# Moving four precomputed weight sums between VectorE and GpSimd, and undoing a split product, in an attention + GEGLU kernel

## The chip, the cores and the metric

The kernel runs on one core of one Trainium2 chip. A core has TensorE (PE, matrix products into PSUM), VectorE (DVE), ScalarE (ACT), GpSimd (POOL), and SyncE (SP), which issues most of the transfers. The engines run side by side, each through its own list of instructions in a fixed order, and wait for each other by semaphores. The metric is the device time of one execution in microseconds. Beside it there is one profiled execution, from which all durations here are taken; its positions are microseconds from the start of its span.

## The reference

Eight batches of attention whose softmax stands on q (over the head's 64 columns) and on k (over the sequence), so that no sequence x sequence matrix arises, and then a gated feed-forward block on the result:

```
q_s = softmax(q, axis=-1);  k_s = softmax(k, axis=2)     # (8, 8, 576, 64)
kv  = einsum('bhsd,bhse->bhde', k_s, v)
x   = einsum('bhsd,bhde->bhse', q_s, kv)                  # -> (4608, 512)
out = (gelu(x @ w_gate) * (x @ w_val)) @ w_out            # 512 -> 1536 -> 512
```

Inputs and output are float32; the kernel multiplies in float16 and adds up in float32.

## The kernel before

**Tiling.** The work goes in nine blocks of 512 rows of x: blocks 0 to 7 are the first 512 of the 576 rows of each batch, and a block 8 (called B) gathers the remaining 64 rows of every batch. The order is 0 to 6, then 8, then 7. x is kept transposed, as `xt` (4 groups of 128 columns by 512 rows). The 1536 hidden columns are 12 groups of 128 (`fi`), and the gated result is `ht`.

**Products.** Blocks 0 and 1 compute gate and value plainly (`ffn_fi`): four matmuls of 512 columns into `psg`, four into `psv`, then GELU on ScalarE (line 471) and the gating on VectorE (line 472), which writes `ht`. From block 2 on, the hidden groups 0 to 5 use Strassen's scheme in Winograd's form (`product_gv`, line 605: seven products instead of eight), and the others stay plain. The output product is plain in block 0 (`mm_out`), and in Winograd's form from block 1 on (`out_strassen` with `product`, line 712).

**Sums for Winograd's form.** They need sums of quarters of each factor, all in float16 in SBUF:

- `sum_w(i)`, line 556: four sums of quarters of w_out into `tw1` to `tw4`, each 128 x 1536 elements, made once. `tw2` reads `tw1`, `tw4` reads `tw2`; `tw3` reads w_out alone. Product 5 reads `tw1`, product 6 `tw2`, product 7 `tw3`, product 4 `tw4`.
- `sum_wgv(nm, i)`, line 586: the same for w_gate and w_val, 128 x 768 elements each. Sums 1, 2 and 4 go to `ws`; sum 3 is written in place into the weights (`wg_sb`, `wv_sb`), which is allowed only once the plain products of block 1 have read these columns for the last time; block 2's seventh product reads them.
- `sum_h`, line 575: the sums of `ht` in each block (`sh`, `s4`, and one in place in `ht`).

**The output stage of block 1.** `out_strassen` runs products 1, 2, 5, 6, 3, 7 and 4 of 12 matmuls with 256 columns each, in three PSUM tiles `psa`, `psb`, `psc`. Between them VectorE scales `psa` or `psc` into SBUF (`snap`, line 744) and adds them into the output tile `yo` (`add`, line 750). Product 4 is added into `psa` after the last add has read it. At fixed places the stage takes in work for other blocks: at place (1, NS, 2), between products 6 and 3, the `kv` products of block 2 (`pskv`, line 342; normalised on VectorE, lines 346 and 348) and the casts of v of batch 3 on GpSimd (line 188); at place (1, NS, 4), in front of product 4, x of block 2 (`unit_x4`, lines 429 and 439), evacuated by ScalarE and VectorE (lines 190 and 192) into `xt` and `xtr`. The first gate product of block 2 reads `xt` right after product 4.

**What sets the order.** Nothing is planned by a scheduler: each engine's order is the order of the calls. A table `plan`, filled by `at(block, kind, index, ...)`, names the places. `ride` calls what stands at a place: FI is a step of the hidden groups of blocks 0 and 1, NS a step of the output stage, PR a step of the later blocks. At NS 17 of block 0, in its last output rows, stand `sum_w(1)` and `sum_w(3)` on GpSimd; at FI 4 of block 1 `sum_w(2)` and `sum_w(4)` on VectorE; at FI 11 of block 1 both in-place sums on GpSimd. The local value `cut` in `out_strassen` splits product 3: in blocks 1 to 5 its last group of `ht` (two matmuls) comes after product 7.

Of the kernel before, what the change touches and what calls it, by code (L numbers as in the profile page):

```python
# [18 lines left out]
def kernel(  # L19
# [10 lines left out]
    nc = tc.nc  # L30

    B, H, S, D = q.shape
# [4 lines left out]
    NFI = F // P  # L37
# [11 lines left out]
    NO = NFI // 2  # L49
# [30 lines left out]
    def big(shape, dt, name, hold=False, seed=False):  # L80
        tag = ring.pop(next(i for i, x in enumerate(ring) if x in full) if seed else 0)
        t = ps_big.tile(shape, dt, name=name, tag=tag)
        words = 1
        for n in shape[1:]:
            words *= n
        (full.add if words == 512 and shape[0] == 128 and dt == f32 else full.discard)(tag)
        if hold:
            held[id(t)] = (t, tag)
        else:
            ring.append(tag)  # L90
        return t

    def let_go(t):
        ring.append(held.pop(id(t))[1])
# [26 lines left out]
    for i, nm in enumerate("gv"):  # L121
        n = 3 * NO * P
# [442 lines left out]
    def sum_h(j0, j1, which, eng="dve"):  # L565
        step = 1 if j1 - j0 == 2 else NO // 2
        js, ks = slice(j0, j1, step), slice(NO + j0, NO + j1, step)
        a11, a21 = ht[:, js, 0:256], ht[:, js, 256:512]
        a12, a22 = ht[:, ks, 0:256], ht[:, ks, 256:512]
        s1, s2 = sh[1][:, js], sh[2][:, js]  # L570
        for i in which:
            o, a, b, op = {1: (s1, a21, a22, ALU.add), 2: (s2, s1, a11, ALU.subtract),
                           3: (a21, a11, a21, ALU.subtract),
                           4: (s4[:, js], a12, s2, ALU.subtract)}[i]
            (nc.gpsimd if eng == "pool" else nc.vector).tensor_tensor(out=o, in0=a, in1=b, op=op)  # L575

    def sum_wgv(nm, i, k=0, n=NO // 2, eng="dve"):
        w = wg_sb if nm == "g" else wv_sb  # L580
        lo, hi = slice(k * P, (k + n) * P), slice((k + NO // 2) * P, (k + NO // 2 + n) * P)
        a11, a21, a12, a22 = w[:, 0:2, lo], w[:, 0:2, hi], w[:, 2:4, lo], w[:, 2:4, hi]
        t = [ws[(nm, k // NO)][:, j, :, k % NO * P:(k % NO + n) * P] for j in range(3)]
        o, a, b, op = {1: (t[0], a21, a22, ALU.add), 2: (t[1], t[0], a11, ALU.subtract),
                       3: (a21, a11, a21, ALU.subtract), 4: (t[2], a12, t[1], ALU.subtract)}[i]
        (nc.gpsimd if eng == "pool" else nc.vector).tensor_tensor(out=o, in0=a, in1=b, op=op)

    def sum_x(xt, xs=xs):
        b11, b12, b21, b22 = (xt[:, c:c + 2, r:r + 256] for c in (0, 2) for r in (0, 256))
# [112 lines left out]
    def product(i, ps, first, ts=(0, 1), js=range(NO)):  # L702
        for j in js:
            for t in ts:
                c0, c1 = slice(t * P, (t + 1) * P), slice(256 + t * P, 256 + (t + 1) * P)
                a = {1: ht[:, j, c0], 2: ht[:, NO + j, c0], 3: s4[:, j, c0], 4: ht[:, NO + j, c1],
                     5: sh[1][:, j, c0], 6: sh[2][:, j, c0], 7: ht[:, j, c1]}[i]
                w = {1: wo_sb[:, j, 0:256], 2: wo_sb[:, NO + j, 0:256],
                     3: wo_sb[:, NO + j, 256:512]}.get(i)
                if w is None:  # L710
                    w = tw[{4: 4, 5: 1, 6: 2, 7: 3}[i]][:, j]
                nc.tensor.matmul(ps[t], a, w, start=(first and j == js[0] and (  # L712
                    t == ts[0] or ps[t].tensor is not ps[ts[0]].tensor)),
                                 stop=(j == js[-1]), skip_group_check=True)

    def get_x(b):
        return get_xt(b) if b < B else xtr

    def last_js(b):
        return (NO - 2 if b < 2 else NO // 2 - 1, NO)  # L720

    def out_strassen(b, last):
        yo = [yop.tile([P, 2, C], f32, name="yo", tag="yo") for _ in range(2)]
        c = (slice(0, 256), slice(256, 512))
        ps, tiles_ = {}, {}

        def get(nm):
            if last:
                tiles_[nm] = [big([P, 256], f32, "ps" + nm, True) for _ in range(2)]
                ps[nm] = [x for x in tiles_[nm]]  # L730
            else:
                tiles_[nm] = [big([P, 2, 256], f32, "ps" + nm, True)]
                ps[nm] = [tiles_[nm][0][:, t] for t in range(2)]

        def parts(nm):
            return [(0, ps[nm][0]), (1, ps[nm][1])] if last else [(slice(0, 2), tiles_[nm][0])]

        def snap(nm):
            sn = ffn.tile([P, 2, 256], f32, name="sn", tag="gl")
            for n, (t, src) in enumerate(parts(nm)):  # L740
                if n:
                    nc.scalar.activation(out=sn[:, t], in_=src, func=ACTF.Copy, scale=1.0 / _H_SCALE)
                else:
                    nc.vector.tensor_scalar(out=sn[:, t], in0=src, scalar1=1.0 / _H_SCALE,
                                            scalar2=None, op0=ALU.mult)
            return sn

        def add(nm, sn, half, col):
            for t, src in parts(nm):
                nc.vector.scalar_tensor_tensor(  # L750
                    out=yo[half][:, t, c[col]], in0=src, scalar=1.0 / _H_SCALE,
                    in1=sn[:, t], op0=ALU.mult, op1=ALU.add)

        js = (0, 1, 2, 3, 4, 5) if b < 2 else (0, 3, 1, 4, 2, 5)
        get("a")
        product(1, ps["a"], True, js=js[:4])
        ride(b, NS, 0)
        if b >= B - 1:
            pair_step(b, get_x(b), NFI - NO // 2 - 1, 4)
        ride(b, PR, "e")  # L760
        get("b")
        product(1, ps["a"], False, js=js[4:])
        sum_h(*last_js(b), (1, 2))
        s1 = snap("a")
        product(2, ps["b"], True, js=js)
        add("b", s1, 0, 0)
        for x in tiles_["b"]:
            let_go(x)
        sum_h(*last_js(b), (4,), "pool" if b > 1 else "dve")
        get("c")  # L770
        product(5, ps["c"], True, js=js)
        sum_h(*last_js(b), (3,), "pool" if b > 1 else "dve")
        s5 = snap("c")
        ride(b, NS, 1)
        product(6, ps["a"], False, js=js)
        s2 = snap("a")
        ride(b, NS, 2)
        cut = NO - 1 if b < B - 2 else NO
        product(3, ps["c"], False, js=js[:cut])
        if cut < NO:  # L780
            product(7, ps["a"], False, js=js)
            add("a", s5, 1, 1)
            product(3, ps["c"], False, js=js[cut:])
        add("c", s2, 0, 1)
        for x in tiles_["c"]:
            let_go(x)
        store_rows(b, 0, yo[0])
        if last:
            finish_last(b, ps["a"], yo[1], s5)
            return  # L790
        if cut == NO:
            product(7, ps["a"], False, js=js)
            add("a", s5, 1, 1)
        ride(b, NS, 4)
        if b == B:
            go_on(B - 1, get_x(B - 1), 1)
        product(4, ps["a"], False, js=js)
        nc.scalar.activation(out=yo[1][:, :, c[0]], in_=tiles_["a"][0], func=ACTF.Copy,
                             scale=1.0 / _H_SCALE)
        let_go(tiles_["a"][0])  # L800
        store_rows(b, 1, yo[1])
# [97 lines left out]
    FI, NS, PR = range(3)  # L899
    plan = {}  # L900

    def at(b, kind, i, *fns):
        plan.setdefault((b, kind, i), []).extend(fns)

    L = lambda f, *a: (lambda: f(*a))

    def load_2nd():
# [6 lines left out]
    at(0, NS, 5, L(unit_t, 1, 0))  # L914
    at(0, NS, 16, L(unit_kv, 1, 0), L(cast_v, 1, 4, 8), L(load_batch, 2, ((v, "v"),)),
       L(norm, 1, 3))
    at(0, NS, 17, L(unit_x, 1, 0, "act", True), L(unit_x, 1, 1, "act", True), L(sum_w, 1, "pool"),
       L(sum_w, 3, "pool"))
    at(0, NS, 7, L(exp, "q", 2))
    first1 = [[L(unit_t, 1, 1), L(unit_kv, 1, 1)],  # L920
              [L(unit_x, 1, 2, "dve"), L(preload, ACTF.Gelu)],
# [8 lines left out]

    at(1, FI, 2, L(unit_trem, 1))
    at(1, FI, 3, L(norm, 2, 2, "pool"), L(load_batch, 3, ((q, "q"), (k, "k"))))
    at(1, FI, 4, L(exp, "k", 2, 0, 4), L(norm, 2, 3, "pool"), L(sum_w, 2), L(sum_w, 4), make_s)
    at(1, FI, 5, L(cast_v, 2, 0, H))
    at(1, FI, 8, L(unit_td, 2))
    at(1, FI, 11, L(exp, "k", 2, 4, 8), L(exp, "q", 3))
# [3 lines left out]
    load_2 = lambda n: load_batch(n, ((v, "v"), (q, "q"), (k, "k")))  # L940
    for i, x in enumerate(("g1", "v1", "g2", "v2", "g4", "v4")):
        at(0, FI, 5 + i, L(sum_wgv, x[0], int(x[1])))
    at(1, FI, NFI - 1, L(sum_wgv, "g", 3, 0, NO // 2, "pool"), L(sum_wgv, "v", 3, 0, NO // 2, "pool"))
    for b in range(2, B):
        n = b + 1
        if n < B:
# [10 lines left out]
    for b in range(2, B - 1):  # L957
        n = b + 1
# [16 lines left out]
    def ride(b, kind, i):  # L975
        for fn in plan.get((b, kind, i), []):
            fn()

    for b in order:
# [16 lines left out]
        if b == 0:  # L996
# [5 lines left out]
            for ns in range(4):  # L1002
                cut = 9 if ns == 2 else 7 if ns == 3 else NFI
# [37 lines left out]
```

The softmax here doesn't subtract the row's maximum and nothing guards it: scores larger than these inputs give would overflow.

## Time and profile before

| | us |
|---|---|
| median of 4 runs (297.27 to 297.55) | 297.37 |
| the profiled execution | 297.45 |
| its span, first to last instruction | 295.5 |
| TensorE busy / VectorE / GpSimd / ScalarE | 286.0 / 220.9 / 200.4 / 181.9 |
| TensorE, VectorE busy from 60 to 71 us (block 1's hidden groups) | 11.00, 10.82 |
| TensorE, VectorE, GpSimd busy from 71 to 76 us (block 1's output) | 4.75, 4.81, 0.00 |
| TensorE, VectorE, GpSimd busy from 76 to 84 us (to block 2's start) | 7.78, 6.26, 4.50 |

The granted clock of TensorE is 1.00 in all these stretches. A line of the timeline reads: start, duration, engine, line of the kernel, operation, output<-inputs by name, shapes, count of merged instructions, and in brackets the idle time of the engine in front of it with what ended it. Successive instructions of one engine overlap a little in the records[...]. A matmul's record includes its drain: in a row of matmuls the distance from start to start is the pace.

### The profile page before, as it was taken

What the parts mean: (1) busy time and instruction counts of PE and PEld (TensorE: products, weight loads), DVE (VectorE), ACT (ScalarE), POOL (GpSimd) and SP (SyncE); (2) the same over time, 40 slices, a digit from 0 to 9 for tenths busy, and PEclk for the clock granted to TensorE, in tenths of its full rate; (3) what the DMA queues carried; (4) which work ended last, traced back from release to release, by engine and by line L of the source; (5) the groups of instructions that cost most, each with busy time, mean ns of one, the idle gap of its engine ahead of it and who ended that gap; (6) DMA issues with size and microseconds to landing.
All of it is one profiled execution on the core that took longest, in us unless ns stands there. A gap on an engine that the chain in (4) does not pass through costs nothing. (4 is left out here: it accounts for less than half of the span.)

```text
span 295.5 us, 6184 instructions
## 1 busy us (share of the span) xinstructions
PE 286.0 (97%) x2401; PEld 198.5 (67%) x2401; DVE 220.9 (75%) x409; ACT 181.9 (62%) x295; POOL 200.4 (68%) x181
## 2 busy tenths in 40 slices
PE   3999999999999999999999999999999999999994
PEld 1544445445866686668666866687667888888884
DVE  2955779999778677867777676777677788958892
ACT  3763367776676668667756966695662477327640
POOL 1557747894386877687768776967886366673770
PEclk9999999999999999999999999999999999999999
DMA  6999999998069504980399029901140110033003
GB/s 220 373 382 389 400 391 392 329 325 231 3 211 389 113 3 156 364 192 3 137 347 246 2 97 342 274 2 73 71 89 12 71 74 2 1 73 71 2 0 144
DMA packets 54621, 51.72 MB, mean 175 GB/s; under 512 B 18496, under 2 KB 50496, under 8 KB 54592
## 3 DMA queue, kind: packets, MB, share of 16 engines
q1 hardware_dynamic: 52864, 49.49, 52.8%
q10 hardware_dynamic: 1728, 1.84, 1.9%
q8 instruction: 19, 0.31, 0.4%
q14 instruction: 10, 0.08, 0.1%
HBM read 37.75 MB, written 9.44 MB: 160 GB/s over the span
## 5 line engine op out<-in xcount | busy, mean ns | idle before, releaser
L466 PE MATMUL psg<-xt,wg_sb 128*128 128x512 f16 x216 | 57.8, 379 | 0.2 <-DVE xt L192 0.2
L466 PE MATMUL psv<-xt,wv_sb 128*128 128x512 f16 x216 | 57.4, 379 | 0.0
L249 POOL TENSOR_TENSOR eq<-eq,rrq 128x640 f16<-128x640 f16 (+1 forms) x27 | 34.7, 1304 | 19.7 <-DVE rrq L242 16.1
L712 PEld LDWEIGHTS <-ht 128*128 128x128 f16 x384 | 36.5, 98 | 8.8 <-issue 2.5
L466 PEld LDWEIGHTS <-wv_sb 128*128 128x128 f16 x216 | 21.0, 98 | 20.5 <-issue 1.2
L466 PEld LDWEIGHTS <-wg_sb 128*128 128x128 f16 x216 | 21.1, 98 | 18.6 <-issue 0.2
L575 POOL TENSOR_TENSOR s<-ht,sh 128x512 f16<-128x512 f16 x21 | 25.3, 1206 | 9.5 <-DVE sh L575 9.5
L575 POOL TENSOR_TENSOR ht<-ht 128x512 f16<-128x512 f16 x21 | 25.2, 1199 | 5.5 <-DVE sh L575 5.5
L605 PEld LDWEIGHTS <-wv_sb 128*128 128x128 f16 x216 | 20.9, 98 | 11.2 <-issue 1.8
L188 POOL CAST v<-vt 128x640 f16<-128x640 f32 x26 | 20.7, 839 | 8.7 <-PE pskv L342 7.1
L650 POOL TENSOR_TENSOR ht<-eq 128x512 f16<-128x512 f32 x12 | 15.4, 1283 | 16.0 <-ACT eq L648 15.8
L471 ACT ACTIVATE gl<-psg 128x512 f32<-128x512 f32 x24 | 13.8, 597 | 16.6 <-PE psg L466 14.2
L630 ACT ACTIVATE glq<-pgb 128x256 f32<-128x256 f32 x27 | 10.2, 379 | 21.9 <-PE pgb L605 14.0
L712 PE MATMUL psa<-tw,ht 128*128 128x256 f16 x192 | 23.4, 272 | 0.0
L212 ACT ACTIVATE ek<-kt 128x1280 f16<-128x1280 f32 (+1 forms) x11 | 19.1, 1748 | 6.1 <-DMA kt<-in_k_dram 4.1
L605 PEld LDWEIGHTS <-wg_sb 128*128 128x128 f16 x216 | 21.1, 98 | 2.5
L660 ACT COPY pgb<-pga 128x512 f32<-128x512 f32 x27 | 15.8, 584 | 9.8 <-PE pga L605 9.5
L472 DVE SCALAR_TENSOR_TENSOR ht<-psv,gl 128x512 f16<-128x512 f32 x24 | 16.0, 683 | 7.2 <-PE psv L466 7.2
L622 ACT ACTIVATE gl<-psg 128x512 f32<-128x512 f32 x30 | 17.7, 589 | 5.7 <-PE psg L466 5.7
L240 DVE TENSOR_REDUCE rq<-eq 128x20 f32<-128x1280 f16 (+1 forms) x12 | 17.1, 1427 | 4.5 <-ACT eq L212 4.5
L712 PEld LDWEIGHTS <-sh 128*128 128x128 f16 x192 | 18.8, 98 | 2.4 <-issue 0.3
L212 ACT ACTIVATE eq<-qt 128x2560 f16<-128x2560 f32 (+2 forms) x10 | 18.4, 1863 | 2.8 <-DMA qt<-in_q_dram 2.8
(164 smaller groups left out, 685.6 us busy)
## 6 DMA issues: line engine op xcount, KB each, us to landing
out_dram<-yo SPq DMA_DIRECT2D x15, 512.0 KB, 3.5
kt<-in_k_dram SPq DMA_DIRECT2D x7, 640.0 KB, 9.0
vt<-in_v_dram SPq DMA_DIRECT2D x7, 640.0 KB, 5.8
qt<-in_q_dram SPq DMA_DIRECT2D x7, 640.0 KB, 7.7
qt<-in_q_dram SPq DMA_DIRECT2D x8, 512.0 KB, 8.3
wost<-in_moe_w_out_dram SPq DMA_DIRECT2D x6, 512.0 KB, 7.9
kt<-in_k_dram SPq DMA_DIRECT2D x6, 512.0 KB, 9.7
vt<-in_v_dram SPq DMA_DIRECT2D x6, 512.0 KB, 6.2
```

Source lines behind the costliest of these rows:

```text
L188: nc.gpsimd.tensor_copy(out=dst, in_=src)
L212: nc.scalar.activation(out=dst[:, n0:NC, h0 * D:h1 * D].rearrange(o, d=D, **({"t": 2} if b >= QUAD else {})), in_=heads(tiles[(nm, b)], b, ...
L240: nc.vector.reduce_sum(rq, e, axis=mybir.AxisListType.X)
L249: (nc.gpsimd if eng == "pool" else nc.vector).tensor_tensor(out=e, in0=e, in1=rrq.unsqueeze(-1).to_broadcast((P, n, 2, D)), op=ALU.mult)
L466: nc.tensor.matmul(ps, w[:, ci, fi * P:(fi + 1) * P], xt[:, ci, :], start=(ci == 0), stop=(ci == HP - 1))
L472: nc.vector.scalar_tensor_tensor(out=ht[:, fi, :], in0=psv, scalar=_H_SCALE, in1=gl, op0=ALU.mult, op1=ALU.mult)
L575: (nc.gpsimd if eng == "pool" else nc.vector).tensor_tensor(out=o, in0=a, in1=b, op=op)
L605: nc.tensor.matmul(ps[:, t], a, x, start=(first and t == 0 and c == 0), stop=(c == 1), skip_group_check=True)
L622: nc.scalar.activation(out=live[c], in_=t, func=ACTF.Gelu)
L650: (nc.vector if k == NFI - NO // 2 - 1 else nc.gpsimd).tensor_tensor(out=ht[:, k:k + NO // 2 + 1:NO // 2, 256:512], in0=cc[:, :, 0], in1=c ...
L660: nc.scalar.copy(out=pb, in_=pa)
L712: nc.tensor.matmul(ps[t], a, w, start=(first and j == js[0] and (t == ts[0] or ps[t].tensor is not ps[ts[0]].tensor)), stop=(j == js[-1]), ...
```

## The change

1. The first sum of w_out goes from GpSimd in block 0's last output rows to VectorE at FI 10 of block 0.
2. The second goes from VectorE at FI 4 of block 1 to GpSimd at NS 17 of block 0, behind the third, which takes the first place there. The fourth stays.
3. The two in-place sums of w_gate and w_val go from GpSimd at FI 11 of block 1 to VectorE at NS 2 of block 1, behind the normalising of kv. The argument `eng` of `sum_wgv` goes with it.
4. `cut` no longer splits product 3 in block 1: all twelve matmuls and the add of `psc` come before product 7 and the add of `psa`.

```diff
-    def sum_wgv(nm, i, k=0, n=NO // 2, eng="dve"):
+    def sum_wgv(nm, i, k=0, n=NO // 2):
...
-        (nc.gpsimd if eng == "pool" else nc.vector).tensor_tensor(out=o, in0=a, in1=b, op=op)
+        nc.vector.tensor_tensor(out=o, in0=a, in1=b, op=op)
...
-        cut = NO - 1 if b < B - 2 else NO
+        cut = NO - 1 if 1 < b < B - 2 else NO
...
-    at(0, NS, 17, L(unit_x, 1, 0, "act", True), L(unit_x, 1, 1, "act", True), L(sum_w, 1, "pool"),
-       L(sum_w, 3, "pool"))
+    at(0, NS, 17, L(unit_x, 1, 0, "act", True), L(unit_x, 1, 1, "act", True), L(sum_w, 3, "pool"),
+       L(sum_w, 2, "pool"))
...
-    at(1, FI, 4, L(exp, "k", 2, 0, 4), L(norm, 2, 3, "pool"), L(sum_w, 2), L(sum_w, 4), make_s)
+    at(1, FI, 4, L(exp, "k", 2, 0, 4), L(norm, 2, 3, "pool"), L(sum_w, 4), make_s)
...
-    at(1, FI, NFI - 1, L(sum_wgv, "g", 3, 0, NO // 2, "pool"), L(sum_wgv, "v", 3, 0, NO // 2, "pool"))
+    at(0, FI, NFI - 2, L(sum_w, 1))
+    at(1, NS, 2, L(sum_wgv, "g", 3), L(sum_wgv, "v", 3))
```

## The prediction

> **What bounds the kernel now.** I read the page's busy times first, then the timeline of TensorE, then those of VectorE and GpSimd around TensorE's stalls.
>
> ```profile
> PE 286.0 (97%) x2401; PEld 198.5 (67%) x2401; DVE 220.9 (75%) x409; ACT 181.9 (62%) x295; POOL 200.4 (68%) x181
> ```
>
> TensorE is busy 286.0 of 295.5 us, and most of the rest is the start. So the change can only gain where TensorE stalls, and lose where it makes it stall. From block 1 on, the waits view gives TensorE two stalls that name another engine:
>
> ```profile
> 72.15 1.25 PE L712 MATMUL psb<-wo_sb,ht 128*128 128x256 f16 x10
> 73.66 0.39 PE L712 MATMUL psb<-wo_sb,ht 128*128 128x256 f16 x2 [0.25 <-DVE ht L472]
> 73.89 1.47 PE L712 MATMUL psc<-tw,sh 128*128 128x256 f16 x12
> 75.20 1.47 PE L712 MATMUL psa<-tw,sh 128*128 128x256 f16 x12
> 82.15 0.90 PE L466 MATMUL psg<-xt,wg_sb 128*128 128x512 f16 x3
> 83.27 0.38 PE L466 MATMUL psg<-xt,wg_sb 128*128 128x512 f16 x1 [0.22 <-DVE xt L192]
> ```
>
> The columns are start, duration, engine, line, operation, count, and in brackets the idle time before it. By these brackets at most 0.25 + 0.22 = 0.47 us can be won. But a matmul's bar also shows its drain. Twelve of 256 columns start every 75.20 - 73.89 = 1.31 us, or 0.109 us each; so the eleventh of product 2 was due at 72.15 + 10 x 0.109 = 73.24 and came at 73.66, 0.42 us late. Matmuls of 512 columns in block 1 come every 0.216 us (four in 0.86 to 0.87), so the fourth psg was due at 82.15 + 3 x 0.216 = 82.80 and came 0.47 us late. Here the Trainium skill's trace page ("Perfetto Trace Analysis", Identifying the Most-Contended Engine) is weighed: it says that matmul busy time misleads because matmuls are pipelined. The idle row would cap the gain at 0.47 us (0.16%); the starts[...] cap it at 0.89 us (0.30%). I take the starts: the weight load before the first late matmul shows 0.53 us of idle time, not 0.25.
>
> Why VectorE is late:
>
> ```profile
> 60.65 2.89 DVE L556 TENSOR_TENSOR tw<-wo_sb,tw 128x1536 f16<-128x1536 f16 x2
> 67.18 1.26 DVE L575 TENSOR_TENSOR ht<-ht 128x512 f16<-128x512 f16 x1
> 68.36 1.85 DVE L575 TENSOR_TENSOR s<-ht,sh 128x512 f16<-128x512 f16 x1
> 72.92 0.68 DVE L472 SCALAR_TENSOR_TENSOR ht<-psv,gl 128x512 f16<-128x512 f32 x1
> 66.34 1.81 POOL L586 TENSOR_TENSOR wg_sb<-wg_sb 128x768 f16<-128x768 f16 x1
> 68.11 1.82 POOL L586 TENSOR_TENSOR wv_sb<-wv_sb 128x768 f16<-128x768 f16 x1
> ```
>
> The gate that the stall waits for starts at 72.92, though its matmuls ended at 71.01: 1.9 us of backlog. The two L575 sums took 1.26 and 1.85 us where the same shape takes 0.42 at 70.85: each ended 0.28 us after a GpSimd weight sum ended (68.15, 69.93). Two-input f16 sums on VectorE and GpSimd instructions exclude each other here.
>
> **The change, part by part.** No DMA is added or removed, and the order on SP, ScalarE and its table loads stays; GpSimd's casts keep their order. All the moves are below.
>
> (1) First sum of w_out to block 0. VectorE would be free for it at about 36.4, after the last wsv sum (35.94 + 0.55); its inputs, the first three w_out casts, end at 35.65. It costs 0.96 us (the shorter of the two L556 on VectorE), GpSimd being idle until 38.72. It ends at 37.4, and the gate behind it, at 37.06 before, starts 0.3 us later. Cover: VectorE then sits idle for 1.58 us, and that gate's ht is first read in the second half of block 0's output, after 24 matmuls x 0.216 = 5.2 us. Price: 0; without cover, 0.3 us.
>
> (2) GpSimd at 48.85 makes the third and second sum instead of the first and third: same shapes, 3.67 + 3.09 us before, so no change. Its new input from (1) is 11 us old by then; the reader of its result, the fourth sum, runs at 60.65. Price 0.
>
> (3) VectorE in block 1 loses one of the two L556. The fourth sum now starts at 60.65 and ends at 61.61. In the old run it stood second and waited for GpSimd's normalisation (1.90 instead of 0.96 us). Saved: 0.96 + 0.94 = 1.90 us.
>
> (4) The in-place sums leave GpSimd at 66.34. That removes the two waits on VectorE: 0.84 + 1.43 = 2.27 us. With (3) that is 4.17 us against a backlog of 1.9 us: gate 11 is made at about 71.1, and the stall of 0.42 us goes. TensorE then runs 0.42 us earlier from 73.24 on.
>
> (5) The same two sums now stand on VectorE behind kv, in front of both L750 adds and the evacuations of the next block's x. These lines are the stretch before:
>
> ```profile
> 77.08 2.71 POOL L188 CAST v<-vt 128x640 f16<-128x640 f32 x4 [7.15 <-PE pskv L342]
> 77.89 0.42 DVE L348 TENSOR_TENSOR kv<-pskv,rck 128x256 f16<-128x256 f32 x1
> 79.97 0.69 DVE L750 SCALAR_TENSOR_TENSOR yo<-psa,sn 128x512 f32<-128x512 f32 x1 [1.66 <-PE psa L712]
> 80.58 0.68 DVE L750 SCALAR_TENSOR_TENSOR yo<-psc,sn 128x512 f32<-128x512 f32 x1
> 81.17 0.72 DVE L192 CAST xtr<-psxr 128x128 f16<-128x128 f32 x2
> 81.93 1.29 DVE L192 CAST xt<-psx 128x512 f16<-128x512 f32 x2
> ```
>
> VectorE idles 1.66 us there, but four GpSimd casts lie beside it. The nearest row is block 6, which already has these two sums and a whole third product, with GpSimd quiet:
>
> ```profile
> 230.94 0.55 DVE L586 TENSOR_TENSOR wg_sb<-wg_sb 128x768 f16<-128x768 f16 x1
> 231.41 0.55 DVE L586 TENSOR_TENSOR wv_sb<-wv_sb 128x768 f16<-128x768 f16 x1
> 231.88 0.68 DVE L750 SCALAR_TENSOR_TENSOR yo<-psc,sn 128x512 f32<-128x512 f32 x1
> 232.95 0.69 DVE L750 SCALAR_TENSOR_TENSOR yo<-psa,sn 128x512 f32<-128x512 f32 x1 [0.40 <-PE psa L712]
> ```
>
> For sums beside casts there is block 2:
>
> ```profile
> 109.81 0.95 DVE L586 TENSOR_TENSOR kt<-kt,wg_sb 128x768 f16<-128x768 f16 x1
> ```
>
> Here the sum ends 0.41 us after the cast that it waited for (110.35), and a cast that waits for a sum ends 0.58 us after it. Whenever both waited, the one that had waited longer got in (68.15, 110.35), so they alternate. The Trainium skill ("SBUF — State Buffer", Who interferes with whom) states it as a lock: a VectorE instruction with two SBUF inputs and a GpSimd instruction that reads SBUF block each other wholly, the first to issue first. That speaks against this part, and block 6's row alone would miss it. Worked out, all 0.42 us earlier than before: pskv done, reciprocal at 77.05; kv at 77.25; first sum issued at 77.60. The casts, one every 0.66 us and 0.72 us long, start at 76.66 and 77.32; the second ends at 78.04. Sum to 78.45, third cast to 79.03, second sum to 79.44. The add of psc starts at 79.36 (VectorE starts 0.08 before the last one's end), the add of psa at 79.97.
>
> (6) Third product whole. Two matmuls (0.22 us) move in front of product 7, whose sum psa needs. Product 7 ends at 79.74, before VectorE gets to it at 79.97. Product 4 adds into the same bank and waits for that add: due at 80.83 - 0.42 = 80.41, it starts at 80.66 + 0.05 = 80.71. So a new stall of 0.30 us. Then xtr and xt follow the adds: before, the last xt ended 3.25 us after the first add began (79.97 to 83.22), so 79.36 + 3.25 = 82.61, and 0.05 us later, as it was before, the fourth psg may start: 82.66. TensorE gets there by itself at 80.71 + 1.31 + 0.65 = 82.67. It started at 83.27 before.
>
> **Sum.** -0.42 (first stall) + 0.30 (product 4) - 0.47 (second stall, now covered) = -0.59, or by the clock of the fourth psg 83.27 - 82.67 = 0.60 us. Behind it TensorE has no stall that names something else than work following it, so the 0.60 us should reach the end: 297.45 - 0.60 = 296.85 for the profiled execution. That stands 0.08 above the median, so the median is forecast at 297.37 - 0.60 = 296.77.
>
> **Bounds of the unknown cost.** What the trace doesn't show is this pair of sums amid these casts with two adds behind. If no lock bites (block 6's row): sums end at 78.6, the psa add follows product 7 at 79.82, product 4 starts at 80.56, psg's fourth at 82.52: gain 0.75 us. If the sums get in only after the last cast: see the second rival. A pass-over of the lock is unlikely on the rows above; I take alternation.
>
> **The rivals.**
> (a) No lock: 297.37 - 0.75 = 296.62. For it: block 6. Against: the 0.95 us in block 2.
> (b) Slower: GpSimd's casts, issued back to back, keep VectorE out until the fourth ends at about 79.30. Sums to 79.71 and 80.18, first add at 80.10, fourth psg at 80.10 + 3.30 = 83.40: 0.13 us later than before, 297.50. The end moves one for one with that first add: even at 79.97, slower by 0.2% (0.59 us, about what a measurement of this kernel can tell from no change) at 80.56. For it: two sums and two adds are in one queue in front of product 4 and of x. Against: in every pair of the trace VectorE got in after one cast.
> (c) The change doesn't mend the first stall: gate 11 stays late for another reason. Then the reciprocal is at 77.47, the sums end at 79.86, the first add at 79.78, fourth psg at 83.08: gain 0.19 us, 297.18. Against: 4.17 us freed.
>
> **How the numbers follow.** Alternation 0.50, (a) 0.22, (b) 0.18, (c) 0.10. Alternation sits on the 0.2% line (0.60 against 0.59 us); I give 0.32 of it to faster, since ScalarE's evacuations before x also come earlier, and 0.18 to same. Faster: 0.32 + 0.22 = 0.54. Same: 0.18 + 0.08 + 0.10 = 0.36, with 0.08 of (b). Slower: the other 0.10 of (b). Range: from (a) less a spread of 0.2 us, 296.4, to just above (b), 297.55; the likeliest case's own range is 296.6 to 297.0.
>
> **What would show it.** The bracket at the eleventh matmul of block 1's product 2 gone; the last gate of block 1 at about 71.1; L575 sums in block 1 near 0.42 us; the two L586 on VectorE at about 77.6, with 0.85 and 1.07 us (lock) or 0.55 (none); product 4's first matmul about 0.3 us after it was due; no wait for xt at psg. I am wrong if the first L750 starts after 80, if product 4 starts later than 81, or if a stall appears in block 0.

## The result and the profile after

The changed kernel takes 296.98 us (median of 41 runs), the kernel before 297.37: 0.39 us less, a ratio of 0.9985 (95% interval 0.9981 to 0.9990). Faster, but within the 0.2% that the prediction calls "same"; 0.60 us was forecast. The profiled execution took 297.04 us, with a span of 295.2.

First TensorE's timeline of the changed kernel in the output stage of block 1 (start, duration, engine, line, operation, count, idle time before):

```profile
72.18 1.47 PE L712 MATMUL psb<-wo_sb,ht 128*128 128x256 f16 x12
73.49 1.47 PE L712 MATMUL psc<-tw,sh 128*128 128x256 f16 x12
76.96 1.49 PE L712 MATMUL psc<-wo_sb,s 128*128 128x256 f16 x12
78.28 1.47 PE L712 MATMUL psa<-tw,ht 128*128 128x256 f16 x12
80.72 1.47 PE L712 MATMUL psa<-tw,ht 128*128 128x256 f16 x12 [0.22 <-DVE yo L750]
82.03 1.03 PE L466 MATMUL psg<-xt,wg_sb 128*128 128x512 f16 x4
```

Product 2 is one row of twelve: its stall is gone. Product 5 starts at 73.49 instead of 73.89, product 4 at 80.72 with the new stall, and the four psg matmuls are one row: the fourth starts at 82.03 + 3 x 0.216 = 82.68, 0.59 us earlier than before (83.27). VectorE in the same stretch:

```profile
60.64 0.93 DVE L556 TENSOR_TENSOR tw<-wo_sb,tw 128x1536 f16<-128x1536 f16 x1
66.93 0.42 DVE L575 TENSOR_TENSOR s<-ht,sh 128x512 f16<-128x512 f16 x1
71.14 0.69 DVE L472 SCALAR_TENSOR_TENSOR ht<-psv,gl 128x512 f16<-128x512 f32 x1 [0.37 <-PE psv L466]
77.63 0.85 DVE L586 TENSOR_TENSOR wg_sb<-wg_sb 128x768 f16<-128x768 f16 x1
78.40 1.07 DVE L586 TENSOR_TENSOR wv_sb<-wv_sb 128x768 f16<-128x768 f16 x1
79.39 0.68 DVE L750 SCALAR_TENSOR_TENSOR yo<-psc,sn 128x512 f32<-128x512 f32 x1
79.99 0.67 DVE L750 SCALAR_TENSOR_TENSOR yo<-psa,sn 128x512 f32<-128x512 f32 x1
81.34 1.29 DVE L192 CAST xt<-psx 128x512 f16<-128x512 f32 x2
```

The last gate now waits for its matmuls (0.37 us idle) instead of being 1.9 us late. The two in-place sums take 0.85 and 1.07 us beside the casts, and the adds begin at 79.39 and 79.99.

So block 1 gave 0.59 us. Not all of it reached the end. The waits of TensorE name VectorE's add twice (line, what was waited for, us in total, times, longest):

```profile
PE psa L712 <- DVE yo L750: 0.4, 2, 0.2
```

(That view also lists a wait of 0.4 us for GpSimd at 10.89 us, in `pst`. It lies 25 us before the first moved instruction, and product 1 of block 1 starts only 0.03 us later than before, at 70.87.) One of the two is the product 4 above. The other is in the next block, where product 4 came on time before. The timelines of TensorE and VectorE in block 2, of the kernel before and then of the changed one:

```profile
111.21 0.60 PE L429 MATMUL psx<-eqt,kv 64*64 64x512 f16 x8
111.76 1.47 PE L712 MATMUL psa<-tw,ht 128*128 128x256 f16 x12
109.22 0.55 DVE L586 TENSOR_TENSOR kt<-wg_sb 128x768 f16<-128x768 f16 x1
109.81 0.95 DVE L586 TENSOR_TENSOR kt<-kt,wg_sb 128x768 f16<-128x768 f16 x1
111.02 0.69 DVE L750 SCALAR_TENSOR_TENSOR yo<-psa,sn 128x512 f32<-128x512 f32 x1 [0.26 <-PE psa L712]
```

```profile
110.63 0.60 PE L429 MATMUL psx<-eqt,kv 64*64 64x512 f16 x8
111.39 1.47 PE L712 MATMUL psa<-tw,ht 128*128 128x256 f16 x12 [0.16 <-DVE yo L750]
108.64 1.11 DVE L586 TENSOR_TENSOR kt<-wg_sb 128x768 f16<-128x768 f16 x1
109.78 0.95 DVE L586 TENSOR_TENSOR kt<-kt,wg_sb 128x768 f16<-128x768 f16 x1
110.66 0.68 DVE L750 SCALAR_TENSOR_TENSOR yo<-psa,sn 128x512 f32<-128x512 f32 x1
```

From psx to product 4 it was 0.55 us, and now it is 0.76. The 0.59 us shrink to 111.76 - 111.39 = 0.37 us, and stay there to the end: TensorE's last row on `psa` starts at 288.61 instead of 288.97. The first of block 2's two sums takes 1.11 us instead of 0.55, so the add behind it is late.

### The profile page after: what moved, and what is told of

Read it like the earlier page. It is cut to its first block, busy times and chain, and to the rows that moved or that the text cites. A ratio compares the mean times of both kernels' runs of the same rounds, so it can differ in the third digit from the quotient of the medians.

```text
span 295.2 us, 6183 instructions
## 1 busy us (share of the span) xinstructions
PE 285.1 (97%) x2401; PEld 198.4 (67%) x2401; DVE 220.1 (75%) x411; ACT 181.9 (62%) x295; POOL 195.9 (66%) x179
## 5 line engine op out<-in xcount | busy, mean ns | idle before, releaser
L188 POOL CAST v<-vt 128x640 f16<-128x640 f32 x26 | 20.0, 811 | 12.8 <-PE pskv L342 11.3
```

Source lines behind the costliest of these rows:

```text
L188: nc.gpsimd.tensor_copy(out=dst, in_=src)
```

## The experiments

The questions: which of the moves mends the first stall, what the new place of the in-place sums and the whole product cost, and what turned in block 2. The theory for block 2 was formed from the profile after: VectorE's first sum and GpSimd's third cast ask for the shared port almost at once, and the change reversed who comes first. ("The port" stands for the lock of the prediction's step 5. What the runs show of it is that one of the two instructions waits until the other is done.) Here is the third cast in GpSimd's timeline of the kernel before, and below it that of the changed one:

```profile
109.26 1.09 POOL L188 CAST v<-vt 128x640 f16<-128x640 f32 x1
```

```profile
108.62 0.72 POOL L188 CAST v<-vt 128x640 f16<-128x640 f32 x1
```

Before, the sum was issued 0.04 us ahead of the third cast (109.22 against 109.26), and the cast waited: 1.09 us. After, it was issued 0.02 us behind it (108.64 against 108.62) and waited itself.

**e1: in-place sums back on GpSimd.**

```diff
-    at(1, NS, 2, L(sum_wgv, "g", 3), L(sum_wgv, "v", 3))
+    at(1, FI, NFI - 1, L(sum_wgv, "g", 3, 0, NO // 2, "pool"), L(sum_wgv, "v", 3, 0, NO // 2, "pool"))
```

> The changed kernel with the two in-place sums back on GpSimd at the end of block 1's hidden groups; the other three parts of the change stay. Theory (VectorE's backlog of 1.9 us; the first sum of w_out alone frees 1.9 us, as the fourth no longer waits for GpSimd): gate 11 of block 1 starts at about 72.2 instead of 72.9, just early enough for the eleventh matmul of product 2 (due at 73.24), so the first stall goes although the in-place sums are where they were. Without them in front of the adds, product 4 of block 1 is late by 0.1 us only. Fourth psg of block 2 at about 82.5 (before 83.27, changed 82.68): 0.75 us earlier. Time 296.6 if block 2 gives nothing back, 296.85 if its first sum falls behind a third cast and product 4 is late by 0.2. Rival (taking the in-place sums from GpSimd is what cures the first stall): 0.3 to 0.4 us of stall stay at product 2, time 297.0 to 297.3.

Measured: 296.75 us, ratio 0.9973 (0.9958 to 0.9989) to the kernel before, which, run beside it, had a median of 297.39. The in-place sums and the last gate:

```profile
65.27 1.81 POOL L586 TENSOR_TENSOR wg_sb<-wg_sb 128x768 f16<-128x768 f16 x1
67.04 1.82 POOL L586 TENSOR_TENSOR wv_sb<-wv_sb 128x768 f16<-128x768 f16 x1
72.18 0.68 DVE L472 SCALAR_TENSOR_TENSOR ht<-psv,gl 128x512 f16<-128x512 f32 x1
79.75 0.69 DVE L750 SCALAR_TENSOR_TENSOR yo<-psa,sn 128x512 f32<-128x512 f32 x1 [0.62 <-PE psa L712]
```

The gate at 72.18 is just early enough, and TensorE has no stall at product 2. The add of psa follows its product, and product 4 is late by 0.1 us (80.49). The fourth psg comes 0.82 us earlier than before, of which 0.01 us is an earlier start of the stage; block 2 took 0.21 us back, the case for which 296.85 was expected. The move of the in-place sums wasn't needed for the first stall, and cost block 1 about 0.2 us.

**e2: the whole third product alone.**

```diff
-        cut = NO - 1 if b < B - 2 else NO
+        cut = NO - 1 if 1 < b < B - 2 else NO
```

> The kernel before with the whole third product in block 1 alone. Theory: the first stall stays at 0.42 us; the add of psc at 79.0 comes before the add of psa at 80.2, product 4 is 0.1 us late (80.94), the evacuation of x ends 0.35 us earlier, so fourth psg at 82.9 instead of 83.27: 0.37 us, time 297.0. Rival (the split is there to hide the add and undoing it costs): product 4 late by 0.2 us or more and no gain at psg, time 297.4 to 297.6.

Measured: 297.23 us, ratio 0.9994 (0.9986 to 1.0002): no difference that is certain. Its TensorE:

```profile
72.17 1.25 PE L712 MATMUL psb<-wo_sb,ht 128*128 128x256 f16 x10
73.68 0.39 PE L712 MATMUL psb<-wo_sb,ht 128*128 128x256 f16 x2 [0.26 <-DVE ht L472]
80.95 1.47 PE L712 MATMUL psa<-tw,ht 128*128 128x256 f16 x12
82.25 1.03 PE L466 MATMUL psg<-xt,wg_sb 128*128 128x512 f16 x4
```

The first stall stays, product 4 comes at 80.95 (0.12 us later than before), and psg runs through: its fourth is at 82.90, 0.37 us earlier, as expected. But block 2 took back 0.21 us here too, though nothing but the split had changed, and so the expected 297.0 did not come. So the reversal in block 2 comes from the split, not from how early TensorE is.

**e3: the changed kernel with the split back.**

```diff
-        cut = NO - 1 if 1 < b < B - 2 else NO
+        cut = NO - 1 if b < B - 2 else NO
```

> The changed kernel with product 3 of block 1 split again. Theory: first stall gone (0.42 us), no stall at product 4, since psa is added first at 79.55; but the add of psc and x come later, the last xt at about 82.8, fourth psg at 82.85: 0.42 us earlier than before against 0.59 in the changed kernel. Time 296.95 without a give-back in block 2, 297.15 with one. Rival (product 4's stall of 0.3 us is a pure loss of the whole product): 0.3 us faster than the changed kernel, 296.7.

Measured: 296.91 us, ratio 0.9986 (0.9979 to 0.9992). Product 4 has no stall (80.32), the fourth psg waits again (82.76, 0.22 us idle), block 2 takes nothing back: its first sum was issued at 108.72, 0.05 us ahead of the third cast, and took 0.55 us. Counted from the start of product 1 (70.76 here, 70.87 in the changed kernel, 70.84 before), the fourth psg comes 0.42 us earlier than before, and in the changed kernel 0.62 us. So the whole product gains 0.20 us in block 1 (0.17 expected) and loses 0.21 us in block 2; the rival's 296.7 did not come.

**Why the split reaches into block 2.** The waits that stand in the two compiled programs differ for GpSimd's block 2 in one place, its last sum into `s4` (DVE_49 and PE_49 are the semaphores that VectorE and TensorE count up):

```
before:  L575 TensorTensor s_89<-ht,sh_778 128x2x256 [waits DVE_49,PE_49]
after:   L575 TensorTensor s_89<-ht,sh_778 128x2x256 [waits DVE_49]
```

With the split, the last two matmuls that read block 1's `s4` come after product 7, so GpSimd has to wait for TensorE once more before it overwrites `s4`. With the whole product that wait is not in the program. With two waits to make, GpSimd's sequencer (POOLq) has one more instruction in front of the sum. The traces show it in the kernel before and in e3, e7 and e11, which have the split, and in none of the nine profiles with the whole product. In the kernel before, the list of line 575's instructions between 104 and 106 us (duration in ns, first and last start):

```profile
L575 POOLq EVENT_SEMAPHORE  x1: 17/17/17, 105.6 to 105.6; - x1
```

GpSimd's timeline of the kernel before, and then of the changed one:

```profile
105.72 1.16 POOL L575 TENSOR_TENSOR s<-ht,sh 128x512 f16<-128x512 f16 x1 [1.56 <-DVE sh L575]
```

```profile
105.07 1.16 POOL L575 TENSOR_TENSOR s<-ht,sh 128x512 f16<-128x512 f16 x1 [1.50 <-DVE sh L575]
```

VectorE's sum that it waits for started at 105.15 and 104.57: with the additional wait, GpSimd follows 0.57 us later, without it 0.50. The same holds in all thirteen profiles: 0.57 us in the four with the split, 0.50 to 0.51 in the nine without. GpSimd runs from there to the casts without a pause, so these 0.07 us are what turns 0.04 us behind into 0.02 us ahead.

**e4: block 2's second sum out of the way.**

```diff
-        at(b, NS, 2, L(sum_wgv, x[0], int(x[1]), NO, NO // 2))
+        at(b, NS, 4 if (b, x) == (2, "g2") else 2, L(sum_wgv, x[0], int(x[1]), NO, NO // 2))
```

> The changed kernel, with the second of block 2's two sums moved on VectorE behind the evacuation of the next x (and so out of the way of both adds). Theory (in the changed kernel the first of these sums is issued 0.02 us behind GpSimd's third cast instead of 0.04 us ahead of it, loses the shared port for one cast, and the adds behind it make product 4 late): product 4 of block 2 is at its due time (excess 0.1 instead of 0.32 us), and the 0.59 us of block 1 reach the end: 296.75, 0.22 us faster than the changed kernel. Rival (the give-back is not from the sums but from something else that is late in block 2): product 4 of block 2 stays 0.2 us late, time 296.98 as in the changed kernel.

Measured: 296.83 us, ratio 0.9980 (0.9972 to 0.9989). The first sum still loses the port, but only one stands in front of the adds:

```profile
108.72 1.10 DVE L586 TENSOR_TENSOR kt<-wg_sb 128x768 f16<-128x768 f16 x1
110.51 0.69 DVE L750 SCALAR_TENSOR_TENSOR yo<-psa,sn 128x512 f32<-128x512 f32 x1 [0.69 <-PE psa L712]
111.25 1.47 PE L712 MATMUL psa<-tw,ht 128*128 128x256 f16 x12
```

The add waits for TensorE, and product 4 follows psx (110.71) by 0.55 us as before the change. The 0.15 us against the changed kernel are less than the 0.22 us expected, but the intervals overlap; in the profile block 2 takes nothing back.

**e5: without the four casts of batch 3.** Left out is the cast of v, so from block 3 on the attention is that of other data.

```diff
-... L(load_batch, 3, ((v, "v"),)), L(cast_v, 3, 0, H))
+... L(load_batch, 3, ((v, "v"),)))
```

> The changed kernel without the four casts of batch 3's v on GpSimd beside the two in-place sums (left out: the attention of block 3 then uses the v of batch 2). It measures what the port costs in block 1. Theory: both in-place sums take 0.55 us instead of 0.85 and 1.07; the add of psc starts at 78.6, the add of psa follows product 7 at 79.82; product 4 at 80.56 instead of 80.72, fourth psg at 82.52 instead of 82.68: 0.15 us gained, 296.83, with block 2's give-back of 0.22 us still in it. Rival (the sums' mere place in front of the adds is what makes product 4 late): product 4 stays at 80.7, time 296.98.

Measured: 296.78 us, ratio 0.9982 (0.9975 to 0.9988). The price of the port in block 1:

```profile
77.74 0.55 DVE L586 TENSOR_TENSOR wg_sb<-wg_sb 128x768 f16<-128x768 f16 x1
78.20 0.55 DVE L586 TENSOR_TENSOR wv_sb<-wv_sb 128x768 f16<-128x768 f16 x1
79.90 0.69 DVE L750 SCALAR_TENSOR_TENSOR yo<-psa,sn 128x512 f32<-128x512 f32 x1 [0.55 <-PE psa L712]
80.65 1.47 PE L712 MATMUL psa<-tw,ht 128*128 128x256 f16 x12
```

From pskv's reciprocal (77.18) to product 4 it is 3.47 us; with the casts it was 80.72 - 77.07 = 3.65. The port costs 0.18 us there (0.16 forecast). The place of the sums in front of the adds costs nothing: in e1, where they are not in this stretch, it is 3.47 us as well (77.02 to 80.49).

**e6: both edits, e1 and e4 (diffs as above).**

> The changed kernel with the in-place sums back on GpSimd (as in the run with that alone) and block 2's second sum behind the evacuation of x. Theory: the two gains add up: block 1 gives 0.75 us and block 2 gives nothing back: 296.55 to 296.65, better than the changed kernel by 0.4 us. Rival (with TensorE earlier still, another wait takes the place of block 2's): 296.75, as without the second edit.

Measured: 296.58 us, ratio 0.9975 (0.9965 to 0.9984); the kernel before, run beside it, had 297.36. The gains add up, TensorE has no wait on another engine after block 0's start, and this is the fastest version that keeps the kernel's work as it is: 0.78 us below the kernel before, by medians 0.40 below the changed one.

**e7: only the two w_out moves.** That is e1's edit and e3's together on the changed kernel.

> Only the moves of the first and second sum of w_out (parts 1 and 2): in-place sums on GpSimd and product 3 split as before. Theory: gate 11 at about 72.2 is early enough, so the first stall of 0.42 us goes; the stall at the fourth psg stays at 0.47; block 2 doesn't flip, since the split leaves GpSimd its additional wait on TensorE: 0.42 us, 296.95. Rival (both the w_out sum and the in-place sums must go to cure the first stall): 297.2 or more.

Measured: 296.93 us, ratio 0.9986 (0.9979 to 0.9992).

```profile
72.22 0.68 DVE L472 SCALAR_TENSOR_TENSOR ht<-psv,gl 128x512 f16<-128x512 f32 x1
82.88 0.38 PE L466 MATMUL psg<-xt,wg_sb 128*128 128x512 f16 x1 [0.22 <-DVE xt L192]
108.84 0.55 DVE L586 TENSOR_TENSOR kt<-wg_sb 128x768 f16<-128x768 f16 x1
108.88 1.09 POOL L188 CAST v<-vt 128x640 f16<-128x640 f32 x1
```

First stall gone, second there, block 2 not reversed, all as expected. These two moves alone give as much as the whole change (296.98).

**e9: one needless memset on GpSimd in block 2.**

```diff
+    at(2, NS, 1, lambda: nc.gpsimd.memset(tiny[:, 2:3], 0.0))
```

> The changed kernel with one memset of a single column more on GpSimd in block 2, in front of its casts: work that nobody needs. Theory (block 2's give-back hangs on which of two instructions, VectorE's first sum or GpSimd's third cast, is issued first, 0.02 us apart): the memset holds GpSimd back by some 0.05 to 0.1 us, the sum gets in first and takes 0.55 instead of 1.11 us, product 4 of block 2 is on time: 0.2 us faster than the changed kernel, 296.77. Rival (not the order of issue but the length of the queue decides): 296.98 or slower.

Measured: 297.03 us, ratio 0.9990 (0.9982 to 0.9998). The theory's number missed:

```profile
107.30 0.10 POOL L974 MEMSET tiny<- 128x1 f32 x1
107.34 3.04 POOL L188 CAST v<-vt 128x640 f16<-128x640 f32 x4
108.65 1.15 DVE L586 TENSOR_TENSOR kt<-wg_sb 128x768 f16<-128x768 f16 x1
108.66 0.73 POOL L188 CAST v<-vt 128x640 f16<-128x640 f32 x1
```

The memset held the casts back by 0.04 us only, and 0.01 us ahead was not enough for the sum. The time is the rival's, but since the order was not clearly turned, this run did not decide.

**e10: three memsets.** As e9, but three of them.

> As the run with one memset, but with three, since one held GpSimd back by 0.04 us only and left the sum 0.01 us ahead of the third cast, which was not enough. In the three kernels where the sum won the port, it was issued 0.04 to 0.05 us ahead. Theory (issue order, with a margin between 0.01 and 0.04 us, decides): three memsets hold GpSimd back by 0.12 us or more, the sum is ahead by some 0.09 us and takes 0.55 us, product 4 of block 2 is on time (excess 0.1 instead of 0.32 us), and the kernel is 0.2 us faster than the changed one: 296.77. Rival (something other than the order of issue kept the sum out): the sum takes 1.1 us again, 297.0.

Measured: 296.63 us (7 runs), ratio 0.9974 (0.9963 to 0.9985).

```profile
107.14 0.41 POOL L974 MEMSET tiny<- 128x1 f32 x3
108.49 0.85 DVE L586 TENSOR_TENSOR kt<-wg_sb 128x768 f16<-128x768 f16 x1
108.88 1.05 POOL L188 CAST v<-vt 128x640 f16<-128x640 f32 x1
```

The three held GpSimd back by more than forecast (the first cast 0.42 us after the first memset), so the sum met the second cast and took 0.85 us, not 0.55; but it was ahead of the third cast, which now waited, and product 4 of block 2 was on time (111.03, 0.55 us after psx). Work added to an engine made the kernel faster, by 0.36 us against the changed kernel run beside it (296.99). Block 2 accounts for 0.21 of that (0.55 instead of 0.76 us from psx to product 4). In the two profiles the rest is an earlier start, of 0.15 us at product 1 of block 1 (70.73 against 70.87), before any of the memsets; with 7 runs it is not shown to be more than spread.

**e11: only the in-place sums on VectorE.** On the kernel before:

```diff
-    at(1, FI, NFI - 1, L(sum_wgv, "g", 3, 0, NO // 2, "pool"), L(sum_wgv, "v", 3, 0, NO // 2, "pool"))
+    at(1, NS, 2, L(sum_wgv, "g", 3), L(sum_wgv, "v", 3))
```

> Only the in-place sums moved to VectorE behind kv (part 3): w_out sums and the split of product 3 as before. Theory: the two waits of 0.84 and 1.43 us go, which is enough by itself for gate 11 (about 71.1 to 71.3), so the first stall goes; the split lets psa's add come first and product 4 is on time; the stall at the fourth psg stays at 0.4 to 0.47: 0.42 us in all, 296.95, as with the w_out moves alone: the two moves cure the same stall and don't add up. Rival (each cures a part): a stall of 0.2 us stays at product 2, 297.15.

Measured: 296.89 us, ratio 0.9980 (0.9972 to 0.9989). Gate 11 is at 71.01, the first stall is gone, the second stays. Each of the two moves cures the first stall alone; together they don't add up.

**e12: the changed kernel again.**

> The changed kernel once more, beside the others of this call. Theory: 296.98, with the first sum of block 2 behind the third cast, 1.1 us long, and product 4 of block 2 late by 0.2 us, since these follow from the order of the program and not from chance. Rival (the order of issue in block 2 is a matter of chance from run to run): the profile may show the sum at 0.55 us, and the times fall into two groups 0.2 us apart.

Measured: 296.99 us, ratio 0.9985 (0.9979 to 0.9992). The sum was issued at 108.90, the third cast at 108.88, and the sum took 1.11 us: the same order as in the first profile. In none of the eight profiles with the whole product (after, e1, e2, e4, e5, e6, e9, e12; e10 with its three memsets set apart) did block 2's first sum win; in all four with the split (before, e3, e7, e11) it won, being 0.04 to 0.05 us ahead. In seven of the eight it was 0.02 to 0.03 us behind, in e9 0.01 us ahead. The order follows from the program. What does vary is the start: in this profile TensorE is 0.29 us later than before already at 45.7 us, which accounts for the 297.23 us of this one execution.

## Why the prediction was right and wrong

- **The first stall** (step 4): right. 0.42 us forecast; product 5 started 0.40 us earlier, with a start that was 0.03 us later. The starts had sized this stall rightly, the bracket of 0.25 us had not. That both moves were counted against the backlog (4.17 us) hid that either is enough (e7, e11).
- **VectorE behind kv** (step 5): right to 0.04 us. The sums ended at 78.48 and 79.47 (forecast 78.45 and 79.44), the adds began at 79.39 and 79.99 (79.36 and 79.97). The lock of the port, with the one that has waited longer getting in, is what e5 took away.
- **The whole product and product 4** (step 6): 80.72 measured, 80.71 forecast; fourth psg 82.68 against 82.67. The second stall was covered as forecast.
- **Block 0** (steps 1 and 2): no stall of TensorE arose around these moves. The first sum took 0.95 us at 36.38, and the gate behind it came at 37.45 instead of 37.06, 0.1 us later than forecast and well within the cover.
- **The sum's last sentence failed**: "Behind it TensorE has no stall that names something else than work following it, so the 0.60 us should reach the end". Block 2 took 0.22 us back. The step looked at TensorE's stalls of the run before, not at how near the next block was to one. Block 2's add of psa had idled 0.26 us, and an add may start 0.08 us before the instruction in front of it ends: 0.34 us of reserve. The sum in front had won the port by 0.04 us. A sum that loses takes 0.56 us longer; 0.56 - 0.34 = 0.22 us.
- **What step 6 left out**: the split also sets when `s4` is read for the last time, and with that a wait in GpSimd's list a block later. The forecast took GpSimd to be untouched there but for the shift.
- With the give-back the sum is 0.59 - 0.22 = 0.37 us; 0.39 was measured. The time lies in the range, but the range (296.4 to 297.55) was wide enough for all the rivals. The favoured case, faster by more than 0.2% (0.54), did not come. "Within 0.2%" had 0.36 because 0.60 us lay on that line and for the sake of the rivals, not because of a loss in a later block; that the result fell there was luck. The path up to block 2's start was not.

**The 1.90 us of step 3** were too much. The instructions did become shorter by about that (2.89 us before, 0.93 us now), but VectorE then stood idle for 1.67 us, waiting for ScalarE, and the next gates began only 0.23 us earlier. Before the change, and after it:

```profile
63.47 1.87 DVE L472 SCALAR_TENSOR_TENSOR ht<-psv,gl 128x512 f16<-128x512 f32 x3
```

```profile
63.24 1.89 DVE L472 SCALAR_TENSOR_TENSOR ht<-psv,gl 128x512 f16<-128x512 f32 x3 [1.67 <-ACT gl L471]
```

In e7, with the w_out moves alone, gate 11 came 0.70 us earlier (72.22), not 1.90. That was enough, since the eleventh matmul of product 2 was due only at 73.24. The forecast of the first stall didn't suffer, because step 4 alone brings gate 11 to its matmuls' end (e11).

## What to carry to other kernels

Where one engine has no gaps, work out the change as a sequence of starts at each stall, and then go on to the next place with the same pattern: if instructions that exclude each other start there within 0.05 us on two engines, treat the order as open and price both. An edit of the order of reads can add or remove a wait on a third engine a block later, so compare the lists of waits and not only the lists of instructions. Moves that cure the same stall don't add up; here the w_out moves or the in-place sums alone gave as much as the whole change (e7, e11), the in-place sums beside the w_out moves cost about 0.2 us (e1), and the whole product lost in block 2 what it won in block 1 (e3). And time saved on an engine is a gain only up to its next wait for another one.

## What was not expected of the hardware

- A lead of 0.01 us in the start that the records show did not win the port for VectorE (e9), one of 0.04 us did (before, e7): somewhere between them lies the turn. Both start in the records just before the second cast ends (109.22 and 109.26 against 109.32 before). The sum as the loser took 0.56 us longer (1.11 instead of 0.55), the cast as the loser 0.37 us (1.09 instead of 0.72).
- A wait that is already fulfilled still costs: one more wait in GpSimd's list moved its next instruction by 0.07 us, though the matmuls that it waits for had ended in block 1, 25 us earlier.
- A memset of one column on GpSimd moved the next instruction by 0.04 us, though its own bar is 0.10 us long (e9: from the start of GpSimd's last sum to that of its first cast it was 1.14 us instead of 1.10); three of them, writing the same column, moved it by 0.42 us (e10: 1.52 us).
